# Retention and multiplicative FFN on one core: the first loads spread over three DMA queues

## The chip, the cores and the metric

The kernel runs on one core of one Trainium2 chip. The metric is device time in microseconds of one execution, as the median of several; a profiled execution stands beside it, with a trace of every instruction and every DMA packet. TensorE is called PE here (PEld is its weight load), VectorE DVE, ScalarE ACT, GpSimd POOL and SyncE SP. A DMA is issued by an engine onto that engine's queue: SP's queue is q1 in the profile, ACT's is q10, and both are of the hardware kind; POOL's is q0, of the software kind. The packets of all three are moved by the core's 16 DMA engines.

## The reference

```python
# B, H, S, D = 8, 8, 576, 64; float32 q, k, v; 4608 tokens, d_model 512, d_ff 1024; float64 weights
scores = scale * np.matmul(q, k.transpose(0, 1, 3, 2))
gamma = 1.0 - 2.0 ** (-5.0 - np.arange(H))
Dmat = np.where(rel >= 0, gamma[:, None, None] ** rel[None, :, :], 0.0)
ret = np.matmul(scores * Dmat, v)
x = ret.transpose(0, 2, 1, 3).reshape(B * S, H * D)
out = ((x @ w1) * (x @ w2) @ w3) @ w_out
```

Retention is attention without a softmax: the scores are weighted by a decay that depends on the distance of two positions, then multiplied by v. Its output is the input of an FFN in which two products are multiplied elementwise.

## The kernel before, in words

**Retention.** The decay is a product of a factor of the row and a factor of the column, so the kernel scales q by `gq` and v by `gk` and needs only a triangular mask. Two batches of eight heads are worked on together, in five chunks of positions: a first short one of 64 (`short`, `sizes[0]`) and four of 128. A chunk g is loaded by `load` (L87 to L95) as tiles `ld_k`, `ld_q`, `ld_v`, with the positions in the partitions and 256 bytes a head and position. `scale` (L195) multiplies q or v by its factors, `front` (L207) transposes k and q on PE (L218) and copies them out of PSUM on ACT (L221), `score` (L224) multiplies them (L233) and masks them on DVE (`pm`, L236), `state` (L240) adds to a running state (L255, copied out at L259), and `pv` (L278) multiplies by v (L299) and hands back the copies that put the result into `xT` (L306). The names k0, q0, v0 stand for chunk 0's tiles here, k1, q1, v1 for those of chunk 1.

**Weights.** They come as float64, in blocks of 512 KB named `raw`. `load_block` (L325) issues a block, five buffers deep; `begin_block` and `end_block` (L374, L408) turn it into float32 in `wA`: three operations on ACT (L395, L396, L397) and four on DVE (L399, L402, L413, L426). The first four blocks are A11, A12, A21, A22 of the Strassen product, called b0 to b3 here. A block with r = 0 (b0, b2) is two DMAs of 256 KB at L342, one for w1 and one for w2; a block with r = 1 (b1, b3) is four DMAs of 128 KB at L345, since each of w1 and w2 is put into the lower and the upper 64 partitions by DMAs of their own (`heads[half]`).

**Order.** All is scheduled by hand: each engine works through its instructions in the order of the program, and so does each DMA queue. SP issues nearly all loads: k0 and q0 (L99, L100), then by L726 to L732 the blocks and chunks in the order b0, v0, b1, k1, q1, b2, v1, b3, and by L744 chunk 2. ACT issues the decay factors of q (`dq`, L98) and those of v (`gk`, L115 and L116); `dq` is transposed on PE into `gq` (L122, L125). POOL builds `ident` and `mask` and scales v0 and v1 (L204).

**Fillers.** `keep_busy(n)` (L127) issues n matmuls of the identity with itself, two passes on PE each, whose result is unused. L118 issues ten at the start.

**The first product.** `up(0, 0, 0, first=True)` (L775) is the first of the FFN. Its first product takes A11 and the tokens of chunks 0 and 1; its second takes S3 (A11 less A21, L149 through L761) and T3 (a difference of tokens, `strassen_tokens`, L496), both made on DVE.

Of the kernel before, what the change touches and what calls it, by code (L numbers as in the profile page):

```python
# [8 lines left out]
F32 = mybir.dt.float32  # L9
# [4 lines left out]
ALU = mybir.AluOpType  # L14
# [5 lines left out]
def kernel(  # L20
# [20 lines left out]
    P = 128  # L41
# [18 lines left out]
    heads = [slice(j * D, (j + 1) * D) for j in range(2)]  # L60
# [3 lines left out]
    ffn = ctx.enter_context(tc.tile_pool(name="ffn", bufs=2))  # L64
# [19 lines left out]

    live = {}

    def load(g, names, engine=nc.sync):  # L87
        i, c = divmod(g, NC)
        sz = sizes[c]
        src = {"k": k, "q": q, "v": v}  # L90
        for nm in names:
            t = pools["ld"].tile([P, 2 * H, D], F32, tag="ld_" + nm, name="ld_" + nm)
            engine.dma_start(
                t[:sz], src[nm][2 * i:2 * i + 2, :, starts[c]:starts[c] + sz, :].rearrange("b h p d -> p (b h) d"))
            live[nm, g] = t  # L95

    dq = ffn.tile([P, 4, 2, TB], F32, tag="c", name="dq", bufs=1).rearrange("p a b s -> p (a b s)")[:H, :S]
    nc.scalar.dma_start(dq, decay_q)  # L98
    load(0, "k")  # L99
    load(0, "q")  # L100

    ident = const.tile([P, P], F32, tag="ident", name="ident")
    make_identity(nc, ident)
# [8 lines left out]
    gk = const.tile([P, NC, H], F32, tag="gk", name="gk")  # L112
    gq = const.tile([P, NC, H], F32, tag="gq", name="gq")
    gqs = const.tile([P, NP, S // 32], F32, tag="gqs", name="gqs")
    nc.scalar.dma_start(gk[:short, 0, :], decay_k[:short, :])  # L115
    nc.scalar.dma_start(gk[:, 1:, :], decay_k[short:, :].rearrange("(c p) h -> p c h", p=P))  # L116
    warm = acc.tile([P, P], F32, tag="acc", name="idle")
    for _ in range(10):  # L118
        nc.tensor.matmul(warm, ident, ident, start=True, stop=True)
    gps = acc.tile([P, NC, H], F32, tag="acc", name="gps")  # L120
    for c in range(NC):
        nc.tensor.transpose(gps[:sizes[c], c, :], dq[:, starts[c]:starts[c] + sizes[c]], ident[:H, :H])  # L122
    for c in (0, slice(1, NC)):
        n = short if c == 0 else P
        nc.vector.tensor_copy(gq[:n, c, :], gps[:n, c, :])  # L125
# [69 lines left out]
    def scale(g, nm, scalar=False, engine=nc.gpsimd):  # L195
        c = g % NC
        sz = sizes[c]
        t, gam = live[nm, g], {"q": gq, "v": gk}[nm]
        t = t[:sz].rearrange("p (b h) d -> p b h d", b=2)
        if scalar:  # L200
            for h in range(H) if scalar is True else scalar:
                nc.scalar.mul(t[:, :, h, :], t[:, :, h, :], gam[:sz, c, h:h + 1])
            return
        engine.tensor_tensor(  # L204
            out=t, in0=t, in1=gam[:sz, c].unsqueeze(1).unsqueeze(3).to_broadcast([sz, 2, H, D]), op=ALU.mult)

    def front(g, names="kq"):  # L207
        c = g % NC
        sz = sizes[c]
        for nm in names:  # L210
            src = live[nm, g]
            dst = pools["fr"].tile([P, 2, NP, P], F32, tag=nm + "T", name=nm + "T",
                                   bufs=1 if nm == "k" and g >= NC else 2)
            for b in range(2):
                tp = acc.tile([P, NP, P], F32, tag="acc", name="tp")
                for p in range(NP):
                    h = b * H + 2 * p
                    nc.tensor.transpose(tp[:, p, :sz],  # L218
                                        src[:sz, h:h + 2, :].rearrange("p a d -> p (a d)"),
                                        ident[:sz, :sz])  # L220
                nc.scalar.copy(dst[:, b, :, :sz], tp[:, :, :sz])  # L221
            live[nm + "T", g] = dst

# [101 lines left out]
    def load_block():  # L325
        n = loaded[0]
        if n == len(blocks):
            return
        key, w = blocks[n]
        t = raw.tile([P, CV, 2], I32, tag="raw", name="raw", bufs=5)  # L330
        if key[0] in ("A", "w12"):
            if key[0] == "A":
                _, r, f = key
                t4 = t.rearrange("p (j c n) t -> p j c n t", j=2, c=2)
                parts = [(t4[:, j], w[:, f * P:(f + 1) * P]) for j, w in enumerate((moe_w1, moe_w2))]
            else:
                _, fp, _, r = key
                parts = [(t.rearrange("p (c n) t -> p c n t", c=2), w[:, fp * QC:(fp + 1) * QC])]
            for t2, src in parts:
                src = src[2 * r * P:2 * (r + 1) * P]  # L340
                if r == 0:
                    nc.sync.dma_start(t2, src.rearrange("(c p) n t -> p c n t", p=P))  # L342
                else:
                    for half in range(2):
                        nc.sync.dma_start(t2[heads[half]],  # L345
                                          src.rearrange("(c a d) n t -> a d c n t", a=2, d=D)[1 - half])
        elif key[0] == "wo":
            src = w.rearrange("(a i x) n t -> i a x n t", i=KF, x=BL)[key[1]]
# [59 lines left out]
    def end_block():  # L408
# [26 lines left out]
        if n >= 4:  # L435
            load_block()
# [32 lines left out]
    def convert_up_to(n):  # L469
        while converted[0] < n:  # L470
            assert go_on() is None
# [252 lines left out]


    load_block()  # L726
    load(0, "v")
    load_block()
    load(1, "kq")
    load_block()  # L730
    load(1, "v")
    load_block()  # L732
    scale(0, "q", engine=nc.vector)
    front(0, "k")
    keep_busy(4)
# [76 lines left out]
    for a in range(2):  # L812
        for f in range(D // BL):
            part = (a * (D // BL) + f) * BL
# [341 lines left out]
    for g in first_pair:  # L1156
        n = (1, 1, 2, 2)[g - NC]
# [7 lines left out]
        half = (n + 1) // 2  # L1165
        if in_blocks[g + 1]:
# [6 lines left out]
            half = 0  # L1173
# [48 lines left out]
    for g in range(2 * NC, G):  # L1222
        n = dealt[g - 2 * NC]
# [87 lines left out]
```

## Time and profile before

| | us |
|---|---|
| median of 3 runs (lowest to highest) | 835.1 (834.79 to 836.32) |
| the profiled execution's own time | 834.5 |
| its span, first to last instruction | 832.8 |
| PE busy in the span | 814.8 (98%) |
| DVE, ACT, POOL busy | 546.3, 291.6, 216.3 |
| k0 issued at 0.81 by SP, on PE transposed at | 5.87 |
| scaling of q0 on DVE begins, ends | 6.77, 7.99 |
| scaling of v0 on POOL begins, ends | 10.13, 12.03 |
| scaling of q1 on DVE begins, ends | 17.91, 19.14 |
| scaling of v1 on POOL begins, ends | 22.48, 24.38 |
| first product of the FFN on PE begins | 28.03 |

The first six rows are of the page and the list of times; the others are from the timeline of the trace, in microseconds from the start of the span. The granted clock of PE is 1.00 in the whole span. A busy share of the DMA engines is the time that their packets took, and packets overlap, so that it can exceed 1.

### The profile page before, as it was taken

The page shows a single profiled execution, that of the slowest core. Times are in us where ns is not written, and L with a number is a line of the kernel's source. Part 1 is how long each engine was busy: PE and PEld are TensorE (multiplying, and loading weights), DVE is VectorE, ACT ScalarE, POOL GpSimd, SP SyncE. Part 2 cuts the span into 40 slices and gives each one's busy share as a digit, 9 for nine tenths or more (in the row PEclk, how much of TensorE's full clock was granted, in tenths as well). Part 3 has the DMA queues.
Part 4 walks back from the last instruction along what each step waited for, and adds up shares of the span by engine and source line. Part 5 has one row for each costly group of instructions (what it writes and reads, how often), then busy time and mean ns, then how long its engine had stood idle before and what let it go on. Part 6 is the DMA issues. An engine that isn't in the chain of part 4 may idle for free.

```text
span 832.8 us, 15818 instructions
## 1 busy us (share of the span) xinstructions
PE 814.8 (98%) x6117; PEld 733.5 (88%) x6117; DVE 546.3 (66%) x962; ACT 291.6 (35%) x609; POOL 216.3 (26%) x247
## 2 busy tenths in 40 slices
PE   7999999999999999999999999999999999999998
PEld 7888999644888998789999889998889998899987
DVE  4899999992554558754657755677745667646653
ACT  4787566581111010245443024341034331033300
POOL 1000000001103262005556005565006460045600
PEclk9999999999999999999999999999999999999999
DMA  9995464436045568998886447978245453145311
GB/s 195 228 215 138 78 153 127 123 105 112 3 80 130 86 175 276 286 282 209 202 227 184 100 85 205 232 232 222 56 92 180 162 191 114 37 150 215 138 30 46
DMA packets 197485, 126.96 MB, mean 152 GB/s; under 512 B 157849, under 2 KB 179097, under 8 KB 197409
## 3 DMA queue, kind: packets, MB, share of 16 engines
q1 hardware_dynamic: 168560, 50.40, 29.4%
q0 software_dynamic: 11824, 63.31, 23.4%
q10 hardware_dynamic: 17024, 12.23, 5.3%
q8 instruction: 48, 0.79, 0.4%
q14 instruction: 29, 0.23, 0.1%
HBM read 103.62 MB, written 22.28 MB: 151 GB/s over the span
## 4 chain that ended last, share of the span: by engine, by line
PE 81%; DVE 7%; DMA 5%; SPq 3%; issue 2%; ACT 2%; POOL 0%; ACTq 0%; DVEq 0%
PE po L645 21%; PE up L1053 17%; PE up L528 14%; PE seed L1053 13%; PE ps L477 7%; PE xps L299 3%; PE sc L233 3%; PE xps L274 1%; DMA out_dram<-ot 1%; PE st L255 1%; SPq L171 1%; DMA bl_k<-in_k_dram 1%; DVE ab L1025 1%; PE tp L218 1%; DMA kept<-wA 1%
## 5 line engine op out<-in xcount | busy, mean ns | idle before, releaser
L645 PE MATMUL po<-w3o,ab 128*128 128x256 f32 x552 | 125.4, 381 | 3.3 <-DVE ot L649 2.4
L645 PEld LDWEIGHTS po<-w3o,ab 128*128 128x128 f32 x552 | 103.6, 190 | 20.4 <-DVE ot L649 4.8
L1058 POOL TENSOR_TENSOR cc<-cc 128x384 f32<-128x384 f32 x112 | 109.3, 1002 | 3.8 <-ACT cc L1076 2.4
L1065 DVE TENSOR_TENSOR cc<-seed,cc 128x384 f32<-128x384 f32 x88 | 48.7, 553 | 69.1 <-PE seed L1053 60.1
L1053 PE MATMUL up<-xT,ra 128*128 128x192 f32 x384 | 73.6, 328 | 0.4 <-DMA ra<-kept 0.4
L181 POOL TENSOR_TENSOR bl_q<-bl_q,gqs 128x512 f32<-128x512 f32 (+1 forms) x26 | 26.0, 1020 | 184.1 <-DMA bl_q<-in_q_dram 180.5
L528 PE MATMUL up<-xT,wA 128*128 128x192 f32 x384 | 70.8, 328 | 0.3 <-ACT xT L306 0.3
L533 DVE TENSOR_TENSOR c<-up,c 128x384 f32<-128x384 f32 x80 | 44.0, 551 | 38.9 <-PE up L528 38.6
L1065 DVE TENSOR_TENSOR cc<-up,cc 128x384 f32<-128x384 f32 x88 | 48.5, 551 | 29.8 <-PE up L1053 21.8
L236 DVE TENSOR_TENSOR pm<-sc,mask 128x512 f32<-128x512 f32 (+1 forms) x80 | 45.3, 628 | 33.4 <-PE sc L233 33.3
L1053 PEld LDWEIGHTS up<-xT,ra 128*128 128x128 f32 x384 | 63.7, 190 | 1.7 <-DMA ra<-kept 0.7
L645 PE MATMUL po<-wB,forms 128*128 128x256 f32 x288 | 65.1, 379 | 0.0
L528 PEld LDWEIGHTS up<-xT,wA 128*128 128x128 f32 x384 | 63.3, 190 | 1.8 <-issue 0.7
L645 PEld LDWEIGHTS po<-wB,forms 128*128 128x128 f32 x288 | 54.7, 190 | 7.4
L1072 ACT COPY seed<-up 128x384 f32<-128x384 f32 x56 | 25.9, 463 | 100.1 <-PE up L1053 59.2
L954 POOL DMA_DIRECT2D ra<-kept x53 | 29.9, 565 | 117.7 <-PE seed L1053 88.5
L477 PE MATMUL ps<-wo,w3T 128*128 128x512 f32 x128 | 55.1, 592 | 0.0
L1053 PE MATMUL up<-ra 128*128 128x192 f32 x288 | 54.8, 326 | 0.0
L1053 PE MATMUL seed<-e,ra 128*128 128x192 f32 x256 | 50.9, 329 | 0.0
L477 PEld LDWEIGHTS ps<-wo,w3T 128*128 128x128 f32 x128 | 24.3, 190 | 30.1 <-issue 29.7
L1053 PEld LDWEIGHTS up<-ra 128*128 128x128 f32 x288 | 48.1, 190 | 0.1
L528 PE MATMUL up<-T,wS 128*128 128x192 f32 x256 | 46.7, 326 | 1.3 <-ACT e L395 1.3
(129 smaller groups left out, 1463.8 us busy)
## 6 DMA issues: line engine op xcount, KB each, us to landing
ra<-kept POOLq DMA_DIRECT2D x53, 896.0 KB, 5.1
raw<-in_moe_w_dram SPq DMA_DIRECT2D x72, 128.0 KB, 3.0
out_dram<-ot ACTq DMA_DIRECT2D x50, 128.0 KB, 2.3
bl_q<-in_q_dram SPq DMA_DIRECT2D x192, 32.0 KB, 3.3
bl_k<-in_k_dram SPq DMA_DIRECT2D x136, 32.0 KB, 3.2
raw<-in_moe_w_dram SPq DMA_DIRECT2D x16, 256.0 KB, 6.1
ld_k<-in_k_dram SPq DMA_DIRECT2D x8, 512.0 KB, 6.3
raw<-in_moe_w_out_dram SPq DMA_DIRECT2D x32, 128.0 KB, 2.7
```

What stands on the lines that cost most here:

```text
L181: nc.gpsimd.tensor_tensor(out=part, in0=part, in1=gqs[:, :, n0:n0 + n].unsqueeze(3).to_broadcast([P, NP, n, BL]), op=ALU.mult)
L233: nc.tensor.matmul(sc[j][:sz, p, :sz], kT[hs, b, p, :sz], qT[hs, b, p, :sz], start=True, stop=True)
L236: nc.vector.tensor_mul(pm[:sz, b, j, :, :sz], sc[j][:sz, :, :sz], mask[:sz, :sz].unsqueeze(1).to_broadcast([sz, NP, sz]))
L477: nc.tensor.matmul(ps, live["w3T", ft][:, g, :], live["wo"][:, g, :], start=(g == 0), stop=(g == KF - 1))
L528: nc.tensor.matmul(ps[:, w, :], a[:, w, r, :], b[:, r, :], start=(new and w == r == 0), stop=(w == r == 1), skip_group_check=True)
L533: nc.vector.tensor_add(c[:, to], ps, c[:, sb])
L645: nc.tensor.matmul(ps[nm], a[A][:, f, :], live["W"][B][:, f, :], start=(f == 0 and not on), stop=(f == NP - 1), skip_group_check=True)
L954: engine.dma_start(ring[n % 3], kept[n % 14 // 7][nm])
L1053: nc.tensor.matmul(ps[:, w, :], weight_of(slot, a, w), B[b], start=(new and w == 0), stop=True, skip_group_check=True)
L1058: nc.gpsimd.tensor_tensor(out=o, in0=o, in1=i, op=ALU.add)
L1065: nc.vector.tensor_add(c[:, j], ps, with_add[:, j])
L1072: nc.scalar.copy(p6, p1)
```

## The change

`load` puts q of a chunk into the last rows of its tile (`rows`), so that q0, which has 64 positions, lies in partitions 64 to 127; for chunks of 128 nothing differs. The factors of q are moved to match: `dq` gets 64 columns of zeros in front (a memset on DVE), the transposes at L122 are all 128 columns wide, and the copies take the right rows. q0 is issued by ACT. v0, `gk`, w2's half of b0 and the upper-partition halves of b1 and b3 are issued by POOL; the half in the lower partitions stays with SP. `gk` comes after v0. The load of b3 stands later in the program, behind the scaling of v0, and one run of fillers has six in place of ten.

```diff
+    def rows(c, nm):
+        lo = P - sizes[c] if nm == "q" else 0
+        return slice(lo, lo + sizes[c])
...
-                t[:sz], src[nm][2 * i:2 * i + 2, :, starts[c]:starts[c] + sz, :].rearrange("b h p d -> p (b h) d"))
+                t[rows(c, nm)],
+                src[nm][2 * i:2 * i + 2, :, starts[c]:starts[c] + sz, :].rearrange("b h p d -> p (b h) d"))
...
-    dq = ffn.tile([P, 4, 2, TB], F32, tag="c", name="dq", bufs=1).rearrange("p a b s -> p (a b s)")[:H, :S]
-    nc.scalar.dma_start(dq, decay_q)
+    dq = ffn.tile([P, 4, 2, TB], F32, tag="c", name="dq", bufs=1).rearrange("p a b s -> p (a b s)")[:H, :P - short + S]
+    nc.vector.memset(dq[:, :P - short], 0.0)
+    nc.scalar.dma_start(dq[:, P - short:], decay_q)
     load(0, "k")
-    load(0, "q")
+    load(0, "q", nc.scalar)
...
-    nc.scalar.dma_start(gk[:short, 0, :], decay_k[:short, :])
-    nc.scalar.dma_start(gk[:, 1:, :], decay_k[short:, :].rearrange("(c p) h -> p c h", p=P))
...
     for c in range(NC):
-        nc.tensor.transpose(gps[:sizes[c], c, :], dq[:, starts[c]:starts[c] + sizes[c]], ident[:H, :H])
+        hi = P - short + starts[c] + sizes[c]
+        nc.tensor.transpose(gps[:, c, :], dq[:, hi - P:hi], ident[:H, :H])
...
-            for t2, src in parts:
+            for part, (t2, src) in enumerate(parts):
                 src = src[2 * r * P:2 * (r + 1) * P]
                 if r == 0:
-                    nc.sync.dma_start(t2, src.rearrange("(c p) n t -> p c n t", p=P))
+                    engine = nc.gpsimd if n == 0 and part else nc.sync
+                    engine.dma_start(t2, src.rearrange("(c p) n t -> p c n t", p=P))
                 else:
                     for half in range(2):
-                        nc.sync.dma_start(t2[heads[half]],
-                                          src.rearrange("(c a d) n t -> a d c n t", a=2, d=D)[1 - half])
+                        engine = nc.gpsimd if n < 4 and half else nc.sync
+                        engine.dma_start(t2[heads[half]],
+                                         src.rearrange("(c a d) n t -> a d c n t", a=2, d=D)[1 - half])
...
     load_block()
-    load(0, "v")
+    load(0, "v", nc.gpsimd)
+    nc.gpsimd.dma_start(gk[:short, 0, :], decay_k[:short, :])
+    nc.gpsimd.dma_start(gk[:, 1:, :], decay_k[short:, :].rearrange("(c p) h -> p c h", p=P))
     load_block()
     load(1, "kq")
     load_block()
     load(1, "v")
-    load_block()
     scale(0, "q", engine=nc.vector)
...
     keep_busy(5)
     scale(0, "v")
+    load_block()
     state(0)
...
     front(1, "k")
-    keep_busy(10)
+    keep_busy(6)
     scale(1, "q", engine=nc.vector)
```

More of the change, by code (lines that the diff above doesn't have):

```diff
@@ L121 @@
     for c in range(NC):
-        nc.tensor.transpose(gps[:sizes[c], c, :], dq[:, starts[c]:starts[c] + sizes[c]], ident[:H, :H])
+        hi = P - short + starts[c] + sizes[c]
+        nc.tensor.transpose(gps[:, c, :], dq[:, hi - P:hi], ident[:H, :H])
     for c in (0, slice(1, NC)):
-        n = short if c == 0 else P
-        nc.vector.tensor_copy(gq[:n, c, :], gps[:n, c, :])
+        n = rows(0 if c == 0 else 1, "q")
+        nc.vector.tensor_copy(gq[n, c, :], gps[n, c, :])
     def keep_busy(n):
@@ L198, in scale @@
         t, gam = live[nm, g], {"q": gq, "v": gk}[nm]
-        t = t[:sz].rearrange("p (b h) d -> p b h d", b=2)
+        n = rows(c, nm)
+        t = t[n].rearrange("p (b h) d -> p b h d", b=2)
         if scalar:
             for h in range(H) if scalar is True else scalar:
-                nc.scalar.mul(t[:, :, h, :], t[:, :, h, :], gam[:sz, c, h:h + 1])
+                nc.scalar.mul(t[:, :, h, :], t[:, :, h, :], gam[n, c, h:h + 1])
             return
         engine.tensor_tensor(
-            out=t, in0=t, in1=gam[:sz, c].unsqueeze(1).unsqueeze(3).to_broadcast([sz, 2, H, D]), op=ALU.mult)
+            out=t, in0=t, in1=gam[n, c].unsqueeze(1).unsqueeze(3).to_broadcast([sz, 2, H, D]), op=ALU.mult)
     def front(g, names="kq"):
@@ L211, in front @@
             src = live[nm, g]
+            n = rows(c, nm)
             dst = pools["fr"].tile([P, 2, NP, P], F32, tag=nm + "T", name=nm + "T",
@@ L218, in front @@
                     nc.tensor.transpose(tp[:, p, :sz],
-                                        src[:sz, h:h + 2, :].rearrange("p a d -> p (a d)"),
-                                        ident[:sz, :sz])
+                                        src[n, h:h + 2, :].rearrange("p a d -> p (a d)"),
+                                        ident[n, n])
                 nc.scalar.copy(dst[:, b, :, :sz], tp[:, :, :sz])
```

## Prediction

> **What bounds the kernel now.** I read the page first, for the engines and the slices.
>
> ```profile
> PE   7999999999999999999999999999999999999998
> DMA  9995464436045568998886447978245453145311
> ```
>
> PE is busy in every slice of 20.8 us but the first, where the DMA engines are busy too. The change touches loads and fillers of the first 25 us alone, so it can win or lose only there. I then took the chain of waits from 15 to 32 us, and DVE's timeline of the same stretch.
>
> ```profile
> 20.62 4.47 DMA raw<-in_moe_w_dram
> 25.20 0.81 ACT e L395
> 26.03 0.73 ACT e L396
> 26.78 0.72 ACT e L397
> 27.51 0.48 ACT xT L306
> 28.03 4.06 PE up L528 x22
> ```
>
> The FFN's first product starts at 28.03 us because b3 lands at 25.09 (20.62 + 4.47), its three ACT operations follow, and `xT`'s copy stands behind them. But this chain is not alone:
>
> ```profile
> 17.91 1.23 DVE L204 TENSOR_TENSOR ld_q<-ld_q,gq 128x1024 f32<-128x1024 f32 x1 [0.41 <-DMA ld_q<-in_q_dram]
> ...
> 21.74 2.48 DVE L236 TENSOR_TENSOR pm<-sc,mask 128x512 f32<-128x512 f32 x4 [0.97 <-PE sc L233]
> 24.14 0.80 DVE L413 SCALAR_TENSOR_TENSOR e<-raw,e 128x512 int32<-128x512 int32 x1
> ...
> 27.54 0.69 DVE L413 SCALAR_TENSOR_TENSOR e<-raw,e 128x512 int32<-128x512 int32 x1 [0.22 <-ACT e L397]
> ...
> 28.88 0.55 DVE L496 TENSOR_TENSOR xT<-xT 128x384 f32<-128x384 f32 x1
> ```
>
> The scaling of q1 waits for its DMA at 17.91. Transposes, scores and the masks of 21.74 hang on it, and from there DVE works without a pause (but 0.22 us) until T3 is made at 29.43. PE's first product is 8 of the 24 passes that take 4.38 us from 28.03, about 1.46 us, so its second product, which needs T3, starts at 29.5, just as T3 is there. Two chains thus end together: b3 and q1. **q1's landing, at about 17.9 us, is the bound that the change must move**; b3 alone, taken forward, gives no more than the 0.22 us. After 29.5 us PE waits rarely until 78 us (0.71 us at 40.08, 1.29 at 54.02, 0.47 at 77.36), and DVE, which is dense there, hangs on PE's products, so a shift at 29.5 is carried to the end.
>
> What sets q1's landing is the stream of loads. Of it I took rates by stretches (columns: busy time and count for PE, PEld, DVE, ACT, POOL; then clock, DMA share, GB/s):
>
> ```profile
> 2.30:16.00 13.70, 11.99 (x166) 11.09 (x166) 6.42 (x13) 7.37 (x13) 1.90 (x1) 1.00 1.20 212
> 3.50:5.00 1.50, 1.50 (x10) 1.50 (x9) 0.00 (x0) 0.46 (x1) 0.00 (x0) 1.00 1.25 166
> 6.00:7.50 1.50, 1.50 (x16) 1.41 (x16) 0.97 (x3) 0.65 (x2) 0.00 (x0) 1.00 1.08 302
> 8.50:10.50 2.00, 1.79 (x41) 1.58 (x39) 1.79 (x5) 1.93 (x4) 0.37 (x1) 1.00 1.16 202
> 11.00:15.50 4.50, 3.38 (x76) 3.08 (x76) 2.57 (x5) 2.54 (x5) 1.03 (x1) 1.00 1.32 222
> 312.00:314.00 2.00, 2.00 (x41) 1.60 (x39) 1.10 (x1) 0.21 (x1) 1.30 (x2) 1.00 1.16 283
> ```
>
> The engines are never idle from 2.3 us on (share over 1), so more queues fill no hole; what can change is the rate. By the order on SP's queue the stretches are: q0 (64 partitions) at 166 GB/s, b0 (128) at 302, b1 (halves of 64) at 202, k1 and q1 (128, 256-byte packets) at 222. The last row is from later, where SP's and POOL's queues move data together: 283.
>
> **The change, part by part.**
>
> *Bytes ahead of q1.* Before: k0, q0, v0 256 KB each, b0, b1, k1, q1 512 KB each, 2.88 MB; at 212 GB/s that is 13.6 us, and the row covers 13.7. After: the same, and b3's POOL half, 0.26 MB: POOL issues it behind the scaling of v0, some 6 us before SP would come to b3. At an unchanged rate q1 lands 0.26 / 0.212 = **1.2 us later**. That is the upper end.
>
> *k0 beside q0.* 0.52 MB in opposite halves of the partitions. q0's 0.26 MB ran at 166; if the pair runs at k0's rate (237 GB/s from 2.5 to 3.5 us), 1.58 us become 1.11: **-0.5**.
>
> *b1's halves beside each other* (SP the lower, POOL the upper partitions). 0.52 MB at 202 is 2.6 us; at b0's 302, 1.7 us: **-0.85**.
>
> *b3's half ahead of q1*, at the two-queue rate of 283: **+0.9**.
>
> *k1 and q1*, 1.05 MB at 222: 4.7 us. Part of them now runs beside POOL's halves. Ends: no gain (222), or 283 throughout (-1.0). I take 250, nearer to their own row: **-0.5**.
>
> *Lag.* k1's and q1's packets are through by about 16 us, but q1 is there at 17.9; some engines are far behind others. Full partitions may even this out: between 0 and -1, taken **-0.4**, nearer to the row of now.
>
> Sum for q1: -0.5 - 0.85 + 0.9 - 0.5 - 0.4 = -1.35. DVE's 0.22 goes too, as b3 now has only two DMAs behind v1 in place of four (0.6 us of issue each): **-1.6 us** at T3. The lower end is all 3.14 MB at 283: 11.1 us against 13.6, -2.5, with lag and DVE -3.1.
>
> *v0 and gk by POOL.* An issue of 64 partitions of v by POOL took 0.86 us and landed after 4.75 (at 454.9 us). POOL is free from 1.6 us; 0.6 for b0's half, then v0 at 2.2, landed by about 7.0, `gk` by 7.5 to 9. The scaling of v0 (1.90) then starts at 7.5 to 9 where it started at 10.13, and the state, `pv(0)` and b1's conversion follow 1 to 2.5 us sooner. Worth nothing by itself: DVE has only 0.41 us of idle before the scaling of q1, and it is q1 that ends it. What POOL issues behind (b1's halves, 0.6 each) stands ahead of that scaling, and is through by 5.5 us. b3's two issues stand ahead of the scaling of v1, which waits till 22.4 anyway.
>
> *q0 by ACT.* ACT's queue: `dq`, then q0 at 1.5 (SP: 1.60), in place of two `gk` issues; the table load behind starts at about 2.2 instead of 2.68. The scaling of q0 can't start before `gq` (6.24, behind the ten fillers), so at most 6.77 - 6.24 = 0.5 us, on chunk 0, with the cover named above. If q0 came late, chunk 0 has about 0.65 us up to the state and 0.41 more on DVE.
>
> *SP* loses q0, v0 and five more issues (about 4 us of issuing), but its queue is full, not its sequencer late: k1 comes to the engines sooner, which is in the sums above.
>
> *Fillers.* Four fewer are eight passes of 0.11 us, 0.9 us, at 17 us, where PE then waits 1.48 us for the scaling of q1: hidden. If q1 comes 1.35 earlier and k1 does not, they would begin to stand in the way; that is why their going is worth nothing by itself. The memset and wider transposes of `dq` are five PE operations of 0.1 us behind fillers, and a DVE memset before DVE's first wait: nothing. If the load of `dq` had to wait for that memset (DVE starts at 0.91), it and q0 behind it on ACT's queue would be 0.2 to 0.4 us late, within q0's cover.
>
> **A rule that speaks against.** The Trainium skill, "DMA: Bandwidth & Descriptors", section "Issuing engines are not separate DMA queues", says that DMAs from several engines run on the same 16 engines and interleave, so that spreading them saves issue time only. By it alone the rate stays 212 and the sum is +1.2 - 0.2. "SBUF — State Buffer" ("Can I just issue two DMAs to hit both halves?") gives only 6% for two DMAs on opposite halves: an estimate of 3.14 MB at 225 GB/s, 14.0 us, +0.4 - 0.2. The 283 GB/s row goes against both, but its mix of transfers is another one. The sum above goes by the rows.
>
> **The rivals.**
>
> 1. *The engines are one server* (chance 0.26): rates stay near 212 to 230, b3's half goes ahead of q1 and takes what was saved. For it: shares of 1.2 to 1.3 in all rows of the opening. Below 3.14 / 13.6 = 231 GB/s on average q1 is late. Price: up to +1.2 - 0.2 = +1.0, 836.1; with half the savings, 835.
> 2. *Two queues give the full 283* (0.17): -2.6 to -3.1, 832.3. Against it: 256-byte packets alone gave 222.
> 3. *PE's clock drops* (0.07), slower than before: fillers end sooner (k1 sooner, 0.9 us cut) while q1 doesn't follow, and the pause before scores grows from 1.5 us (with transposes, 2.8 us without a plain matmul) to 4 or more. The start shows the price: filler passes 0.21 us apart for the first 3.4 us, 0.11 after. Scores and state product (2.06 + 1.10) would take twice that: +3.2, less the gain; 836.7 or more. The longest pause with no such loss in this trace is 1.8 us of PEld; it decides from somewhere above 2.8.
> 4. *POOL's packets crowd out k0 and q0* (0.04): from 312 to 314 us POOL's 96 packets moved 0.31 MB and SP's 1032 moved 0.26, so a turn of POOL's is some 13 times as long. Were b0's half and v0 (0.52 MB) served first, q0 would come 2 us late, 1 us beyond its cover: 836.
>
> **How the numbers follow.** The likeliest case (0.46) is -1.6 us: span 831.2, and the profiled execution's 834.5 becomes 832.9. That run was 0.6 below the median of 835.1; against the median, 833.5, its own range 832.6 to 834.6. The range reaches from rival 2 to rival 1 and the start of 3: 832.0 to 836.6. About 0.2% (1.67 us: from 833.4 to 836.8) is what a measurement can tell. Faster by more: 0.17 and two thirds of 0.46, less what noise takes: 0.45. Slower by more: 3 and a little of 1: 0.12. Within: 0.43.
>
> **What would show it.** Right: q1's scaling starts at 16 to 17 us, PE's second product of `up` at about 28, rates of 240 to 290 GB/s from 3 to 15 us, v0 scaled from 7.5 to 9. Wrong: q1 at 18 or later with rates near 212 (rival 1); PEld of the scores at twice its 0.06 us spacing (3); q0 scaled later than 7.8 (4). A stretch after 30 us in which PE waits for a block or q2 that it had before would undo the gain too.

## The result, and the profile after

| | before | after |
|---|---|---|
| median of 6 runs each, us | 835.2 | 841.52 |
| lowest to highest | 834.34 to 836.32 | 840.6 to 845.26 |
| the profiled execution's own time, its span | 834.5, 832.8 | 844.33, 842.6 |

The changed kernel is **slower**, by less than 1%: the ratio is 1.0082, its 95% interval 1.0066 to 1.0097, so 5.5 to 8.1 us. The forecast was 833.5, and the range ended at 836.6. The profiled execution lies 2.8 us above the median of its kernel, so two more profiles of each kernel were taken later (d1 to d4). The helpers' lines stand 5 to 13 higher after the change: L204 is L211, L218 is L226, L233 is L241, L397 is L408, L413 is L424, L496 is L507.

The engines' slices of the page after:

```profile
PE   8899999999999999999999999999999999999998
PEclk9999999999999999989999999999999999999999
DMA  9994464445035658996876536979255363145401
```

The first digits of PE are hardly other than before, and an 8 stands in PEclk at the 18th slice, where before there were none. The slices are 21 us wide and show neither loss well. The stretches of the opening do (columns: stretch; busy time and count for PE, PEld, DVE, ACT, POOL; granted clock, DMA share, GB/s):

```profile
2.30:16.00 13.70, 11.54 (x84) 10.57 (x84) 4.43 (x10) 4.80 (x8) 5.46 (x8) 1.00 1.13 187
3.50:5.00 1.50, 1.50 (x9) 1.50 (x8) 0.00 (x0) 0.00 (x0) 1.50 (x3) 1.00 1.11 187
6.00:7.50 1.50, 1.50 (x14) 1.48 (x13) 0.36 (x2) 0.15 (x1) 0.00 (x0) 1.00 1.06 237
8.50:10.50 2.00, 1.24 (x6) 0.94 (x5) 0.00 (x0) 0.00 (x0) 0.00 (x0) 1.00 1.08 161
11.00:15.50 4.50, 3.60 (x42) 3.29 (x43) 3.16 (x7) 2.79 (x5) 1.42 (x1) 1.00 1.22 168
```

The opening moved 187 GB/s where it had moved 212. Only the stretch that had held q0 before rose (166 to 187); the other three fell, from 302 to 237, from 202 to 161 and from 222 to 168. The clock column says 1.00 here, but it reads so only because it leaves out the time before the first warming; the filler passes tell more below. From 8.5 to 10.5 us DVE, ACT and POOL do nothing at all. DVE's timeline says what for (start, busy time, engine, line and operation, tiles; in brackets the idle time ahead of it and what ended it):

```profile
10.59 1.22 DVE L211 TENSOR_TENSOR ld_q<-ld_q,gq 64x1024 f32<-64x1024 f32 x1 [3.47 <-DMA ld_q<-in_q_dram]
...
21.57 0.69 DVE L424 SCALAR_TENSOR_TENSOR e<-raw,e 128x512 int32<-128x512 int32 x1 [3.26 <-ACT e L408]
22.30 0.69 DVE L437 SCALAR_TENSOR_TENSOR wA<-m,e 128x512 f32<-128x512 f32 x1
22.91 1.22 DVE L211 TENSOR_TENSOR ld_q<-ld_q,gq 128x1024 f32<-128x1024 f32 x1
...
27.78 2.49 DVE L244 TENSOR_TENSOR pm<-sc,mask 128x512 f32<-128x512 f32 x4 [2.59 <-PE sc L241]
...
34.50 0.55 DVE L507 TENSOR_TENSOR xT<-xT 128x384 f32<-128x384 f32 x1
```

q0, scaled at 6.77 before, is scaled at 10.59 and had waited for its DMA. q1 is scaled at 22.91 (17.91 before) and **no longer waits for its DMA**, which had landed at 20.11: in front of it on DVE stands b1's conversion, which waited 3.26 us for ACT. T3, the end of the chain, is 5.6 us late (34.50 for 28.88). The chain of waits up to there (start, time, what took it) starts at q0:

```profile
1.45 9.05 DMA ld_q<-in_q_dram
...
13.02 1.97 PE sc L241 x32
14.99 2.43 PE idle L137 x10
17.42 1.29 PE st L263 x32
```

PE's scores and fillers in it are long: 1.97 us for the scores of chunk 0 (1.15 before), 2.43 for ten fillers (1.38 before). They ran before the clock was full. In this profile the granted clock is first full from 17.87 us (before: from 4.9), falls to half again from 24.69 to 28.11, and once more from 369.44 to 376.26.

### The profile page after: what moved, and what is told of

The parts are those of the page before. It is cut to its first block, busy times and chain, and to the rows that moved or that the text cites. A ratio compares the mean times of both kernels' runs of the same rounds, so it can differ in the third digit from the quotient of the medians.

```text
span 842.6 us, 15816 instructions
## 1 busy us (share of the span) xinstructions
PE 823.3 (98%) x6109; PEld 740.7 (88%) x6109; DVE 546.4 (65%) x963; ACT 291.9 (35%) x609; POOL 221.6 (26%) x255
## 4 chain that ended last, share of the span: by engine, by line
PE 83%; DVE 6%; DMA 5%; issue 2%; SPq 2%; ACT 1%; POOL 0%; ACTq 0%; DVEq 0%; POOLq 0%
PE po L656 21%; PE up L1066 17%; PE up L539 14%; PE seed L1066 13%; PE ps L488 7%; PE sc L241 3%; PE xps L307 3%; SPq L177 2%; PE xps L282 1%; PE tp L226 1%; PE st L263 1%; DMA ld_q<-in_q_dram 1%; DMA kept<-wA 1%; DVE ab L1038 1%; DMA kept<-wS 1%
## 5 line engine op out<-in xcount | busy, mean ns | idle before, releaser
L967 POOL DMA_DIRECT2D ra<-kept x53 | 29.9, 565 | 122.6 <-PE seed L1066 101.8
L488 PEld LDWEIGHTS ps<-wo,w3T 128*128 128x128 f32 x128 | 24.3, 190 | 30.1 <-issue 29.7
```

The costliest lines, as they stand in the source:

```text
L488: nc.tensor.matmul(ps, live["w3T", ft][:, g, :], live["wo"][:, g, :], start=(g == 0), stop=(g == KF - 1))
L967: engine.dma_start(ring[n % 3], kept[n % 14 // 7][nm])
```

## The experiments

The rows "alone" are edits of the kernel before, the others of the changed kernel. Ratios are to runs of the kernel before on the same chip, whose medians were 836.07, 836.83 and 836.91 us in the three groups of timed runs. Landings, starts and rates are of one profile each; the rate is that of 2.3 to 16 us. "Clock" is the mean granted clock of the timed runs; the kernel before has 0.9970 to 0.9979 in these groups, the changed kernel 0.9930 in its six.

| kernel | ratio, 95% interval | clock | GB/s | q0, q1 landed | v0 scaled | T3 starts |
|---|---|---|---|---|---|---|
| before (three profiles) | 1 | 0.997 to 0.998 | 212, 211, 212 | 6.7, 7.5, 6.7; 17.9 each | 10.1, 11.2, 10.4 | 28.9, 30.6, 29.2 |
| after (three profiles) | 1.0082 (1.0066 to 1.0097) | 0.9930 | 187, 195, 191 | 10.5, 8.6, 8.7; 20.1, 20.4, 19.7 | 14.1, 14.0, 13.2 | 34.5, 33.2, 32.2 |
| s1: q0 by ACT, alone | 1.0044 (1.0030 to 1.0059) | 0.9972 | 211 | 7.3; 18.3 | 10.4 | 29.7 |
| s2: v0 and gk by POOL, alone | 1.0040 (1.0016 to 1.0063) | 0.9951 | 208 | 7.2; 18.3 | 8.9 | 29.3 |
| s3: weights' halves by POOL, alone | 1.0059 (1.0042 to 1.0076) | 0.9932 | 199 | 8.6; 20.2 | 13.4 | 31.2 |
| s4: six fillers, alone | 1.0022 (1.0006 to 1.0039) | 0.9966 | 211 | 7.0; 18.2 | 10.3 | 29.1 |
| a1: after, q0 by SP | 1.0073 (1.0051 to 1.0095) | 0.9933 | 201 | 7.6; 19.9 | 10.8 | 31.4 |
| a2: after, weights by SP | 1.0046 (1.0024 to 1.0067) | 0.9956 | 206 | 8.3; 18.4 | 10.3 | 29.1 |
| a3: after, v0 by SP, gk by ACT | 1.0022 (1.0010 to 1.0033) | 0.9964 | 206 | 9.3; 19.7 | 11.7 | 31.4 |
| a4: after, 14 more fillers | 1.0052 (1.0035 to 1.0069) | 0.9985 | 196 | 8.7; 20.7 | 12.6 | 31.9 |
| b1: after, POOL's loads by ACT | 1.0075 (1.0050 to 1.0100) | 0.9922 | 197 | 7.7; 17.9 | 13.2 | 34.4 |
| b2: after, v0 and gk ahead on POOL | 1.0050 (1.0031 to 1.0070) | 0.9936 | 195 | 8.0; 18.6 | 10.7 | 31.2 |
| b3: before, first fillers 10 to 2 | 1.0028 (1.0017 to 1.0038) | 0.9961 | 201 | 7.6; 19.1 | 11.6 | 29.9 |
| c1: after, weights by SP, more fillers | 1.0031 (1.0017 to 1.0044) | 0.9974 | 209 | 8.3; 17.2 | 10.2 | 30.4 |

No version beat the kernel before. A profile can lie far from its kernel's median: that of s2 is the fastest of ten runs (835.42 us, median 840.09), that of a1 the fastest of six (838.9, median 843.11), that of b1 the fastest of four (839.78, median 842.34).

### The parts alone: s1 to s4

**s1**, q0 in the upper partitions by ACT, with `gk` behind it; the rest as before:

```diff
-    load(0, "q")
+    load(0, "q", nc.scalar)
```

> The kernel before with one part of the change: q0 in the upper partitions, issued by ACT (gk behind it on ACT). Crowding theory (packets of POOL's queue, some 13 times as long a turn, are served ahead of q0 and k0): no POOL traffic, so q0 lands at 6 to 7 us, its scaling starts below 7, and the time is within 1 us of before (834.2 to 836.2). Rate theory (more queues lower the rate of all, as 185 GB/s in place of 212 in the changed kernel's 4 to 14 us): the rate falls here too, q1 is scaled at 18.5 to 19.5, time 836 to 837. Clock theory (PE misses its first warming): nothing here delays chunk 0, so PE is at full clock from about 5 us as before.

Measured: 839.46 us, ratio 1.0044, above every range expected. q0 landed at 7.3, within the scatter of the kernel before (6.7 to 7.5), and T3 at 29.7 too. So this part moved the opening by under a microsecond, and gave nothing of the gain forecast for k0 beside q0. Most of its 3.4 us come later; the section on the stage at 360 us below says where.

**s2**, v0 and `gk` by POOL alone:

```diff
-    load(0, "v")
+    load(0, "v", nc.gpsimd)
+    nc.gpsimd.dma_start(gk[:short, 0, :], decay_k[:short, :])
+    nc.gpsimd.dma_start(gk[:, 1:, :], decay_k[short:, :].rearrange("(c p) h -> p c h", p=P))
```

> The kernel before with v0 and gk issued by POOL, the rest as before. Crowding theory: v0's POOL packets stand against q0 from 3.5 us, q0 lands 0.5 to 1.5 us later (scaled at 7.3 to 8.3), gk late behind v0, time 835 to 837. Rate theory: rate from 3 to 15 us near 195, q1 scaled near 19, time 836 to 837.5. Neither: v0 sooner, time 834 to 835.5.

Measured: 840.09 us (835.42 to 842.79 in ten runs), ratio 1.0040. v0 landed at 8.6 and was scaled at 8.93, inside the 7.5 to 9 that the prediction gave: with the weights left on SP's queue, POOL's queue does bring v0 sooner, and T3 is late by 0.4 us only. As forecast, v0 sooner was worth nothing. But the time is above every range expected, and the profile, 4.7 us below the median, doesn't show where the median's 4.0 us go.

**s3**, the halves of b0, b1 and b3 by POOL alone, b3 at its old place in the program:

```diff
-                    nc.sync.dma_start(t2, src.rearrange("(c p) n t -> p c n t", p=P))
+                    engine = nc.gpsimd if n == 0 and part else nc.sync
+                    engine.dma_start(t2, src.rearrange("(c p) n t -> p c n t", p=P))
...
+                        engine = nc.gpsimd if n < 4 and half else nc.sync
```

> The kernel before with w2's half of b0 and the upper halves of b1 and b3 issued by POOL (0.79 MB), b3 at its old place. Crowding theory: b0's and b1's halves (0.52 MB at 1 to 2 us of POOL's issuing) are served ahead of q0 and v0; q0 scaled at 8 to 10, v0 at 11.5 or later, time 837 to 841. Rate theory: q0 hardly later (below 7.5), q1 scaled at 18.5 to 19.5, time 836 to 837.5.

Measured: 839.98 us, ratio 1.0059. Its opening:

```profile
2.30:16.00 13.70, 12.89 (x111) 11.74 (x112) 5.27 (x11) 4.89 (x8) 4.44 (x6) 1.00 1.15 199
```

The rate fell from 212 to 199 GB/s, q0 (by SP, as before) landed at 8.6, v0 at 13.2 and q1 at 20.2: all the lateness of the changed kernel's q1, by this part alone. It was full-clocked only from 13.99 us on. The ranges of the crowding theory held.

**s4**, six fillers in place of ten before the scaling of q1, alone:

```diff
-    keep_busy(10)
+    keep_busy(6)
```

> The kernel before with keep_busy(6) in place of keep_busy(10) behind the transposes of k1, nothing else. Crowding and rate theories: no change, 834.5 to 836. Clock theory in its strong form (the missing 0.9 us lets the clock fall before the scores of chunk 1): half clock for some 3 us at 19 us, time 836.5 to 838.

Measured: 838.2 us, ratio 1.0022 (1.0006 to 1.0039). The loads are as before and T3 is 0.25 us late, but the clock was at half from 43.03 to 46.44 and from 367.3 to 370.71 in its profile. The half clock that the strong form of the clock theory expected at 19 us did not come there. The four fillers were priced at nothing; 0.5 to 3.3 us is small, but not nothing.

The four parts alone cost 3.4, 4.0, 3.9 and 2.1 us by their medians, 13.4 together, and the whole change 6.3. So these prices are not separate terms that add up. A loss of a common kind that each kernel meets would do this, and the runs below look for it.

### Parts taken back: a1 to a4

```diff
-    load(0, "q", nc.scalar)
+    load(0, "q")
```

> The changed kernel with q0 issued by SP behind k0 (upper partitions kept). Crowding theory: q0 stands in SP's queue ahead of SP's weights, but POOL's packets are still served ahead of it; q0 scaled at 8 to 9.5 instead of 10.59, time 838 to 841. If ACT's queue alone was what lost the turns: q0 scaled below 7.5, time 836 to 838.

**a1** (q0 back on SP) measured 843.11 us, ratio 1.0073: q0 landed at 7.6 again, but q1 at 19.9, and nothing was won; both expectations ended at 841 or below. So q0's lateness, with which the chain of after begins, is not what the whole loss hangs on.

```diff
-                    engine = nc.gpsimd if n == 0 and part else nc.sync
+                    engine = nc.sync
...
-                        engine = nc.gpsimd if n < 4 and half else nc.sync
+                        engine = nc.sync
```

> The changed kernel with all weights by SP (v0 and gk by POOL, q0 by ACT, b3 late, six fillers). Crowding theory: 0.52 MB less ahead of q0 on POOL's queue: q0 scaled at 7 to 8, gk there by 9, time 834.5 to 836.5. Rate theory: rate stays near 190 with three queues, q1 scaled near 20, time 837 to 840.

**a2** (weights back on SP) measured 839.36 us, ratio 1.0046. q1 landed at 18.4, and T3 started at 29.1, 0.2 us behind the kernel before. With s3 this settles, by one profile of each, what delays q1: **it is late with the weights' halves on POOL's queue** (19.7 to 20.7; 18.6 in b2, where they stand later in the queue), **and by under 0.6 us without them**, but for the 19.1 of b3. The time is one that the rate theory expected, with landings nearer to the crowding theory's. But it was still 2.5 us above before; the prediction's chain ends at T3, so this loss is not in that chain.

```diff
+    nc.scalar.dma_start(gk[:short, 0, :], decay_k[:short, :])
+    nc.scalar.dma_start(gk[:, 1:, :], decay_k[short:, :].rearrange("(c p) h -> p c h", p=P))
...
-    load(0, "v", nc.gpsimd)
-    nc.gpsimd.dma_start(gk[:short, 0, :], decay_k[:short, :])
-    nc.gpsimd.dma_start(gk[:, 1:, :], decay_k[short:, :].rearrange("(c p) h -> p c h", p=P))
+    load(0, "v")
```

> The changed kernel with v0 by SP and gk by ACT (behind q0), weights halves still by POOL. Crowding theory: b0's and b1's halves are served ahead of q0, 0.52 MB in place of 0.79: q0 scaled at 8.5 to 10, time 837 to 841. If gk behind v0 on POOL (scaling of v0 at 14.08) was the bound: v0 scaled at 11 to 12, time 836 to 838.

**a3** (v0 on SP, `gk` on ACT) measured 838.33 us, ratio 1.0022, the best of the four, though its profile shows q0 at 9.3 and T3 at 31.4. One profile at 840.68 us, above the kernel's median, isn't a good witness of that median, and the cause of its being the best stays open. The second expectation, that `gk` behind v0 on POOL's queue was the bound, came near: v0 was scaled at 11.7, in place of 13.2 to 14.1.

```diff
-    keep_busy(4)
+    keep_busy(14)
...
-    keep_busy(6)
+    keep_busy(10)
```

> The changed kernel with 14 fillers instead of 4 ahead of q0's transposes and 10 instead of 6 ahead of q1's: PE works on through the wait for q0, so its clock should warm by about 11 us. Clock theory: tp, scores, fillers and state of chunk 0 at half the time, and no half clock at 24.7 to 28.1; time 837 to 839, some 3 to 4 us below the changed kernel. Crowding alone: q0 at 10.6 and gk at 13.9 are the same, time 840 to 841.5.

**a4** (the loads of the change, with fillers in the pauses) measured 841.06 us, ratio 1.0052, with a mean clock of 0.9985, the highest of all kernels; in its profile the clock is full from 4.28 us to the end. The same 32 scores of chunk 0, in a4's timeline of PE:

```profile
11.02 1.15 PE L241 MATMUL sc<-qT,kT 64*64 64x64 f32 x32 [0.21 <-ACT qT L229]
```

take 1.15 us where the first profile of after took 1.97, and T3 starts at 31.9 in place of 34.5. So fillers in PE's pauses do hold the clock, which shows that the pauses lose it. What is left at T3, 3.0 us, is loads and the added fillers themselves. But the time did what "crowding alone" expected (840 to 841.5), and not the clock theory (837 to 839): by the ratios a4 won back 0.0030 of 0.0082, some 2.5 us, and at a clock above that of the kernel before it is still 0.52% slower.

### Queues, order, and the cold start: b1, b2, b3, c1

```diff
-                    engine = nc.gpsimd if n == 0 and part else nc.sync
+                    engine = nc.scalar if n == 0 and part else nc.sync
...
-                        engine = nc.gpsimd if n < 4 and half else nc.sync
+                        engine = nc.scalar if n < 4 and half else nc.sync
...
-    load(0, "v", nc.gpsimd)
+    load(0, "v", nc.scalar)
```

> The changed kernel with everything that it gives to POOL given to ACT instead: two hardware queues, SP and ACT, share the same pieces. If the fall in rate (187 GB/s from 2.3 to 16 us against 212) and the crowding are POOL's packets' own: rate back to 205 to 212, q0, first on ACT's queue, scaled below 7.8, time 836 to 838. If a second stream of any kind does it: rate 185 to 198, q0 below 8 (nothing is ahead of it on ACT) but k1 and q1 late, q1 scaled at 20 to 22, time 838 to 841.

**b1** (all that POOL loads, `gk` too, given to ACT's queue) measured 842.34 us, ratio 1.0075:

```profile
2.30:16.00 13.70, 9.89 (x86) 9.13 (x86) 4.53 (x10) 4.59 (x8) 1.89 (x1) 0.91 1.20 197
```

Two queues of the hardware kind gave 197 GB/s, hardly more than with POOL's (187 to 195), as the expectation for a second stream of any kind had it; the time is above both ranges. q0 and q1 landed at 7.7 and 17.9, near the kernel before, yet q1 was scaled only at 22.7: ACT, which now issues eight loads more, comes late to the copies and conversions of chunk 0. Its table load, ahead of the first copy of kT, starts at 10.68, behind two issues that were held until 9.39; in the kernel before it starts at 2.68. So the rate fell with either second queue that was tried for the weights (though a3 had 206, as a2 had with the weights on SP), and q0 landed later than 7.7 only in kernels with loads on POOL's queue.

```diff
-    load_block()
     load(0, "v", nc.gpsimd)
...
+    load_block()
```

> The changed kernel with v0 and gk issued by POOL ahead of w2's half of b0, nothing else moved. Crowding within POOL's queue: gk, now behind 0.26 MB less, lands 1.5 to 2.5 us sooner (scaling of v0 at 11.5 to 12.5 instead of 14.08), q0 still crowded (9 to 10.5), time 839 to 841. If q0's lateness alone sets chunk 0: 840.5 to 842.

**b2** (v0 and `gk` ahead of b0's half on POOL) measured 841.46 us, ratio 1.0050: v0 scaled at 10.69 and q1 landed at 18.6, 1.0 to 1.7 us sooner than in the changed kernel, but T3 still came at 31.2, with the clock at half from 11.30 to 21.54. So the order within POOL's queue has a part in q1's landing, and doesn't mend the whole. The time is that of the second expectation.

```diff
-    for _ in range(10):
+    for _ in range(2):
```

> The kernel before with 2 fillers instead of 10 at the start, loads untouched: PE has a pause from about 2.3 us until k0's transposes, so its clock should warm at 9 to 15 us instead of 4.9. It measures the price of a late warming by itself. Clock theory: transposes, scores, fillers and state of chunk 0 at twice the time, T3 0.7 to 2.5 us later, time 835.5 to 838.5. If chunk 0's cover takes it all: no change from the kernel before.

**b3** (the kernel before with two fillers at the start) measured 838.94 us, ratio 1.0028 (1.0017 to 1.0038), 1.4 to 3.2 us, with full clock from 13.25 us. That is just above the range expected. It was meant as the price of a cold start with the loads untouched. They did not stay quite untouched (201 GB/s, q1 at 19.1), so it is an upper end of that price.

```diff
-                    engine = nc.gpsimd if n == 0 and part else nc.sync
+                    engine = nc.sync
...
-                        engine = nc.gpsimd if n < 4 and half else nc.sync
+                        engine = nc.sync
...
-    keep_busy(4)
+    keep_busy(8)
...
-    keep_busy(6)
+    keep_busy(10)
```

> The changed kernel without its two suspected harms: all weights by SP, and more fillers (8 instead of 4 ahead of q0's transposes, 10 instead of 6 ahead of q1's). v0 and gk by POOL, q0 by ACT, and the late b3 stay. If POOL's weights and the clock are the whole cause: T3 within 0.5 us of the kernel before, time within 1.5 us of it. If something else of the change costs (v0 or q0 on their queues, the late b3): 1.5 to 4 us above it.

**c1** (weights on SP and more fillers) was expected within 1.5 us of before if POOL's weights and the clock were the whole cause. It measured 839.44 us, ratio 1.0031, 2.5 us slower: **that theory failed as a full account.** In c1 q1 landed at 17.2, 0.7 us sooner than before, the only kernel where this happened; but the clock was full only from 10.96 us, and scaling of q1 came at 19.85, behind chunk 0.

### How far do single profiles scatter: d1 to d4

d1 and d2 are the kernel before, d3 and d4 the changed one, each without an edit.

> The kernel before, unchanged, profiled once more. The theory (loads crowded by GpSimd's weight halves, and a clock that warms late) expects this profile to stay near the first one of before: first q scaled at 6.7 to 7.7 us, second q at 17.9 to 18.6, rate from 2.3 to 16 us of 205 to 212 GB/s. The rival (one profile's scatter is as large as the differences of 0.2 to 1 us read from single profiles) expects the second q to be scaled at 19 us or later, or the first q later than 8, with nothing changed.

> The same as for the run before it: together they give three profiles of the kernel before. If any of them has the half clock between 366 and 376 us, the theory expects it to lose 1 to 3 us there, as the experiments' profiles did, with the opening untouched.

> The changed kernel, unchanged, profiled once more. The theory expects the first q landed later than 9 us, the second q scaled later than 20.5, and a rate from 2.3 to 16 us of 185 to 200 GB/s again; the time of the first full clock may differ. The rival (the first profile was an unlucky one) expects one of them to be back within 1 us of the kernel before.

> The same as for the run before it: a third profile of the changed kernel, for the scatter of its landings and of its first full clock.

One profile each: 835.99 and 835.04 us for the kernel before, 840.28 and 839.25 for the changed one. d2 repeats the first profile of before within some 0.5 us. d1 doesn't: its loads are the same, but PE got its full clock at 14.2 us in place of 4.9, and the scaling of q1 is late with nothing changed:

```profile
18.70 0.69 DVE L413 SCALAR_TENSOR_TENSOR e<-raw,e 128x512 int32<-128x512 int32 x1 [2.80 <-ACT e L397]
20.04 1.22 DVE L204 TENSOR_TENSOR ld_q<-ld_q,gq 128x1024 f32<-128x1024 f32 x1
```

q1 had landed at 17.9, but b1's conversion waits 2.80 us for ACT in front of it, just as after the change. So for differences under 2 us in the opening a single profile of each kernel doesn't do; the rival of the expectation held for the scaling of q1, and the theory for the rates (211 to 212 before, 187 to 195 after); q0, expected later than 9 after the change, landed at 8.6 in d3.

d1 and d4 are a **matched pair**: both cold until 14.2 and 14.4 us, both at full clock from there on. Their openings (d1 first, then d4):

```profile
2.30:16.00 13.70, 13.66 (x133) 12.65 (x134) 6.40 (x13) 5.00 (x9) 1.90 (x1) 1.00 1.19 211
```

```profile
2.30:16.00 13.70, 13.23 (x115) 12.07 (x116) 4.48 (x10) 4.79 (x8) 6.27 (x9) 1.00 1.12 191
```

The span is 834.2 us in d1 and 837.5 in d4. So, by one profile of each, **3.3 us is what the change costs at an equal clock**, and the rest, 6.3 - 3.3 = 3.0 us of the medians, is left for the clock. Of the 3.3 us, 1.6 stand at T3; nearly all of the other half comes behind 372 us (table below), with no clock lost, and its cause stays open. A second pair at full clock to the end, a4 and the first profile of before (from 4.28 and 4.9 us on), is 6.0 us apart (838.8 and 832.8), with 14 fillers more in a4.

The mean clocks give a like share from the other side: 0.9930 against some 0.9975 is 0.0045 of 838 us, up to 3.8 us of full-speed time that was not granted. Less came of it: within a kernel a timed run is on average 0.38 us longer for each 0.001 less of mean clock (a straight line through the 143 timed runs of all these kernels, each set against the mean of its kernel), which makes 0.0045 worth some 1.7 us. So the clock's part is an estimate, 1.7 to 3.0 us of 6.3.

### The stage at 360 us

To see where each profile falls behind, I took the start of the same DVE instruction in each kernel, less its start in the first profile of before (us; the columns are the times in before):

| | 28.9 | 300 | 351 | 366 | 372 | 400 | 830 |
|---|---|---|---|---|---|---|---|
| d1 (before) | 1.7 | 1.1 | 1.7 | 1.6 | 1.6 | 1.6 | 1.4 |
| d2 (before) | 0.3 | 0.3 | 0.9 | 0.5 | 0.5 | 0.5 | 0.5 |
| s1 | 0.8 | 1.5 | 1.6 | 3.0 | 4.0 | 4.0 | 4.1 |
| s2 | 0.4 | 0.2 | 0.7 | 0.3 | 0.3 | 0.9 | 1.2 |
| s3 | 2.3 | 2.5 | 2.9 | 3.0 | 3.0 | 5.0 | 5.2 |
| s4 | 0.3 | 1.5 | 2.2 | 2.7 | 3.9 | 3.9 | 3.7 |
| a1 | 2.6 | 3.1 | 3.6 | 3.4 | 3.4 | 4.0 | 4.4 |
| a2 | 0.2 | 0.3 | 0.8 | 1.9 | 3.4 | 4.0 | 4.3 |
| a3 | 2.5 | 3.2 | 3.6 | 5.3 | 6.5 | 6.5 | 6.4 |
| a4 | 3.0 | 4.8 | 4.8 | 5.0 | 5.0 | 5.7 | 6.0 |
| b1 | 5.5 | 5.7 | 5.7 | 5.4 | 5.4 | 5.4 | 5.3 |
| b2 | 2.3 | 3.4 | 3.5 | 4.5 | 6.0 | 6.6 | 7.0 |
| b3 | 1.0 | 0.7 | 1.8 | 3.3 | 4.6 | 4.6 | 4.4 |
| c1 | 1.5 | 2.6 | 3.0 | 3.4 | 3.4 | 3.9 | 4.3 |
| d4 (after) | 3.4 | 3.0 | 3.5 | 3.4 | 3.4 | 4.3 | 4.8 |
| d3 (after) | 4.3 | 4.2 | 4.9 | 4.4 | 4.4 | 5.0 | 5.8 |
| first profile of after | 5.6 | 5.2 | 5.9 | 6.9 | 8.7 | 9.3 | 9.8 |

What is lost at T3 is kept for 300 us, as forecast, within 0.8 us in most kernels; s4, c1, b2 and a4 lose 1.1 to 1.8 us more on the way. But s1, a2 and b3, little behind there, lose 2.4 to 2.8 us between 351 and 372, and the first profile of after 2.8. The timeline there, first of before:

```profile
350.93 3.60 SPq L895 DMA_DIRECT2D kept<-wA  x4
...
359.77 0.35 ACTq L723 DMA_DIRECT2D out_dram<-ot  x1
360.22 2.45 ACT L202 ACTIVATE ld_q<-ld_q,gq 64x128 f32<-64x128 f32 x8 [2.33 <-DMA kept<-wA]
```

and of after:

```profile
356.88 2.72 SPq L908 DMA_DIRECT2D kept<-wA  x4
...
366.19 0.39 ACTq L734 DMA_DIRECT2D out_dram<-ot  x1
366.69 2.42 ACT L209 ACTIVATE ld_q<-ld_q,gq 64x128 f32<-64x128 f32 x8 [4.91 <-DMA kept<-wA]
...
368.00 0.27 PE L226 MATMUL tp<-ident,ld_q 64*128 64x64 f32 x1 [0.31 <-ACT ld_q L209]
...
369.71 1.97 PE L263 MATMUL st<-ld_v,ld_k 64*64 64x64 f32 x32
```

The chain of waits of after says what ACT waits for:

```profile
357.90 8.21 DMA kept<-wA
366.16 0.04 issue
366.19 0.39 ACTq L734
366.59 0.04 issue
366.64 0.04 issue
366.69 2.43 ACT ld_q L209 x8
```

ACT's store of an output (`out_dram`) starts when one of SP's stores of weights (`kept`) has landed, the third of a run of four, and ACT's scaling of a later q stands behind it in the program. The trace gives both stores the same semaphore, and in the 15 profiles that record this landing ACT's issue starts 0.07 to 0.08 us after it. SP issued that store at 357.90, where before it had been 351.93: 6.0 us later, about the lag of that time, and it took 8.2 us to land in place of 7.8. So the scaling is 6.5 us late, while PE had caught up (k's transposes 4.0 us late, at 366.57 for 362.59); and the transposes of q, which in before had their heads ready, wait 0.3 us for some of them. After these pauses the clock is at half from 369.44 (the state product takes 1.97 us; at full clock it took 1.15).

Of 15 profiles of edited kernels, the three of after included, seven have a half clock that begins between 367 and 371 us (the first of after, s1, s4, a2, a3, b2, b3), and of three of before none. Between 351 and 372 us the seven lose 1.6 to 2.9 us; the other eight, and d1 and d2, between -0.5 and 0.4. That the pauses bring the clock down here is argued from a4 and from the order in time, not shown by a run at this place, and they don't always: the same waits of 0.3 us stand in d3, d4, s3, a1, b1 and c1, whose clock stays full. Why a kernel's store lands later than its lag (s1: 2.6 us later at a lag of 1.6) stays open too.

## Why the prediction was wrong

**The rates: the failed step.** The sum for q1 rested on gains from a second queue: k0 beside q0 -0.5, b1's halves beside each other -0.85, k1 and q1 at 250 GB/s -0.5, lag -0.4, and b3's half at 283 for +0.9. Measured, the rate fell to 187 to 195, below the 212 of before, and q1 landed 1.8 to 2.5 us later in place of 1.35 sooner. The row of 283 from 312 us was of other transfers and didn't carry over, and even rival 1, with an unchanged rate as its worst case (+1.2), was too mild. By its size the rate is enough for that: 3.14 MB at 191 GB/s take 16.4 us, against 13.6 for the 2.88 MB of before, +2.8. But the rate alone doesn't set q1's landing; what is served ahead of it does so as well. By the packets, 3.38 MB had been started when q1 landed in before, at 212 GB/s, and 3.50 to 3.68 MB in after, at 195 to 200. a3 had 213 GB/s up to that moment and q1 still 1.8 us late, behind 3.78 MB; b1 and b2 had 204 and 198 GB/s and q1 at 17.9 and 18.6, with 3.24 and 3.30 MB. Nor is q1's landing the whole of T3's 3.3 to 5.6 us: chunk 0 has a part (below), and in d4 DVE waits 1.93 us for b2 behind it. Here the Trainium skill's rule ("DMA: Bandwidth & Descriptors", section "Issuing engines are not separate DMA queues"), that spreading saves issue time only, was the better guide than my row, and the runs go beyond it: 187 to 206 GB/s in the kernels with halves on a second queue (s3, after, a1, a3, a4, b1, b2), 206 to 212 without, but for one at 201 (b3).

**What POOL's queue takes.** From 4 to 14 us, by the packets of the traces:

| | before | s3 | first profile of after | b1 |
|---|---|---|---|---|
| POOL's queue: KB, packet size, mean time of one | none | 778, 4 KB, 322 ns | 774, 4 KB, 375 ns | none |
| SP's queue: KB | 2137 | 1164 | 851 | 1048 |
| ACT's queue: KB | 16 | 16 | 191 | 921 |

The weights came in packets of 1 KB on SP's and ACT's queues (76 to 87 ns each), but in packets of 4 KB on POOL's (v0 too, in s2), beside the 256-byte packets of q, k and v on the other queues (25 to 31 ns). A byte took about as long in the large packets as in those of 1 KB; a turn took over ten times as long as one of 256 bytes. Rival 4 said this of POOL's packets and gave it 4 in 100. The lateness that it named came: q0 landed 1.9 to 3.8 us behind the 6.7 of the first profile, against the 2 in its price, and the chain of after begins with it. But a1, with POOL's loads unchanged and q0 on SP's queue, had q0 at 7.6, so POOL's packets alone don't make it, and the mechanism is not shown.

**"v0 landed by about 7.0, gk by 7.5 to 9."** They landed at 11.6 to 12.5 and 13.1 to 14.3, and the term was booked as a gain worth nothing. The duration was from an issue at 454.9 us that had POOL's queue to itself; in s2, with the weights left on SP, v0 took 7.0 us from its issue in place of 4.75. In the changed kernel v0 was scaled at 13.2 to 14.1, 3 to 4 us behind the first profile of before:

```profile
14.08 1.90 POOL L211 TENSOR_TENSOR ld_v<-ld_v,gk 64x1024 f32<-64x1024 f32 x1 [8.24 <-DMA gk<-decay_k_dram]
```

The state product comes after it (in d4 it waits for it outright), and ACT's copy of the state and b1's conversion stand behind that, so this too holds back the scaling of q1. a3 and b2, with v0 sooner, have better ratios than the changed kernel (1.0022 and 1.0050); a1, with v0 at 10.8, has not (1.0073), so the price of this term alone stays open.

**The cover of chunk 0: failed.** "0.65 us up to the state and 0.41 more on DVE" was right as a number, and the price of going beyond was not: once chunk 0 is late, b1's conversion on ACT and DVE, behind it in program order, stands before the scaling of q1. d1 shows it with nothing changed: q1 landed at 17.9 and was scaled at 20.04. I took one chain ("q1's landing") as the bound because it was the one that the profile showed ending last; a second one, through chunk 0 and b1, ended 0.4 us earlier.

**The clock: rival 3, under-weighed.** Its price (scores and state at twice their time) was about right, its condition was not. It need not be the pause before q1's scores: PE can miss the first warming (full clock from 17.87 and 14.42 us in two profiles of after), and lose it later (369.44). Its part is an estimate, 1.7 to 3.0 us of the 6.3.

**The fillers "hidden".** s4 says 0.5 to 3.3 us, and not through the 0.9 us of work that was counted: in its profile 1.1 us are lost at 41 us, where PE waits 2.09 us for ACT (0.71 before), 0.9 in the half clock that follows from 43.03, and 1.6 in the stage at 360 us.

**"A shift at 29.5 is carried to the end."** Nearly held for 300 us; at 360 us seven profiles add 1.6 to 2.9 us to it, which no step of the prediction had.

## What to carry to other kernels

Where DMA engines are already at a share over 1, a second queue is a decision on who is served late: price it with the rate of the stretch itself, never with a rate from a stretch with other transfers, and look at packet sizes: here small packets came late beside large ones on another queue. Before a load on the bound is moved, list what stands behind every other load in the same stretch, in program order on each engine; a chain that ends 0.4 us earlier is a bound too. Take two or three profiles of the kernel before: what differs among them (here 1.7 us at T3) is the least that a single profile can tell.

## What the runs showed of the hardware

- Full and half clock alternate in whole windows of 3.41 us (6.83, 10.24), at a phase that differs from run to run. The Trainium skill ("TensorE: Matmul & The Clock Gate", "Part 1: The HAM clock gate") says that the window is free-running; the runs agree, and add a price: the same kernel before had its full clock from 4.85, 4.9 or 14.2 us, and 834.5 to 835.99 us of time with it.
- The same loads on two or three queues moved less than on one: 197 GB/s (SP and ACT, b1) and 187 to 195 (SP, ACT and POOL) against 211 to 212. It is not the only thing that lowers the rate: b3, with the loads of before and fewer fillers, had 201.
- A DMA issue on ACT can hold ACT's arithmetic for microseconds far from the change, until another engine's DMA has landed: at 360 us ACT's store started 0.08 us after an earlier store of SP's with the same semaphore, and ACT had stood still for 2.33 us before the change and 4.91 after.
